# Block decay factors gathered by GpSimd and DMA in place of products on TensorE, and four more blocks transposed by DMA

## The chip, the cores and the metric

The kernel runs on one core of a Trainium2 chip. The metric is the time of one execution on the device in microseconds; lower is better. A ratio in this document is the mean time of one kernel's fast runs over the mean time of the other kernel's fast runs of the same rounds on the same chip, so it is not quite the ratio of the medians that are quoted beside it. A run is called slow here when it lies over 1.5% above the fastest of its kernel.

## The reference

A gated linear attention over 4 batches, 8 heads, 768 steps and a head size of 48, followed by an MLP on the 3072 tokens:

```python
state = alpha[:, :, t, :, None] * state + np.einsum('bhd,bhe->bhde', k[:, :, t], v[:, :, t])
y[:, :, t] = np.einsum('bhd,bhde->bhe', q[:, :, t], state)
...
h = x @ w_in                      # 3072 x 384 by 384 x 2048
r = np.maximum(h, 0.0)
g = s * (r * r) + b
return g @ w_out                  # 2048 x 384
```

`alpha` is drawn between 0.8 and 1.

## The kernel before

The sequence is cut into 24 blocks of 128 steps, six to a batch. A block takes logarithms of alpha, sums them along the block on TensorE (`cum`), and takes two exponentials, `b` and its inverse. VectorE scales q by `b` and k by the inverse. The scaled pair is transposed, on TensorE or by DMA, and gives the block's own output. A product of k and v (`KV`) updates the state. The new state is multiplied by the block's decay factor, one number for each of 384 columns, `blast`:

```python
def st_cum(n):
    la = la_sb[n % 2]
    nc.tensor.matmul(out=cum_ps, lhsT=U_bf, rhs=la[:, :, 0:D], start=True, stop=True)
    if n % NCH == NCH - 1:
        return
    laf = la.rearrange("a h d -> a (h d)")
    for p in range(NP):                      # 4 products with a column of ones
        nc.tensor.matmul(out=bl_ps[:, p : p + 1], lhsT=laf[:, 128 * p : 128 * p + 128],
                         rhs=ones_col_bf, start=True, stop=True)

def st_exp_i(n):
    nc.scalar.activation(out=binv_sb[n % 2], in_=cum_ps, func=AF.Exp, scale=-1.0)
    if n % NCH != NCH - 1:
        nc.scalar.activation(out=blast_sb[n % 2], in_=bl_ps, func=AF.Exp)

def st_vcast(n):                             # GpSimd; KV and the block's output need vp
    nc.gpsimd.tensor_copy(out=vp_sb[n % 4]..., in_=v_in[n % NIN]...)

def st_snew(n):                              # GpSimd; the next block's output needs the state
    ...
    nc.gpsimd.tensor_tensor(out=s_sb[n % 3], in0=t1_sb[n % 2], in1=bl, op=ALU.mult)
```

All these operations, and those of the MLP, are entered in a small planner in the kernel with an engine, a duration, a priority and what they read and write. The planner simulates the engines and writes the program in the order that comes out. On the chip each engine then takes its instructions in that order, whatever the real durations are.

## Time and profile before

| | before |
|---|---|
| time, median | 185.82 us (185.15 to 185.98, 3 runs) |
| span of the profiled execution | 183.4 us |
| TensorE / VectorE / ScalarE / GpSimd busy | 174.6 / 138.7 / 106.0 / 40.2 us |
| transposed on TensorE: blocks 4 to 7; by DMA | 4; 16 |

The prediction shows the main lines. Two more views matter for what came. One is VectorE's product of k by the inverse (busy us, mean ns of one, idle time before it):

```profile
L421 DVE TENSOR_TENSOR qk<-k_in,binv 128x384 bf16<-128x384 f32 x20 | 11.9, 596 | 0.1
```

The other is the list of waits: who waited, for whom, us in total, how often, and the longest.

```profile
POOL s_st L483 <- DVE s_st L472: 46.0, 9, 10.0
POOL vp L410 <- DMA v_in<-in_v_dram: 40.7, 12, 7.5
```

After the start GpSimd has two sorts of work, the state update (`s_st`) and the cast of v (`vp`), and stands idle before both. The second line says that a cast usually sits ready in the queue before its v has been loaded: the casts are early, which costs nothing, and nobody waits for them.

### The profile page before, as it was taken

Reading aid. Unit: us, or ns where it says so; the run is one execution under the profiler, and the core shown is the slowest. Engines: PE = TensorE matmul, PEld = TensorE weight load, DVE = VectorE, ACT = ScalarE, POOL = GpSimd, SP = SyncE. Lnnn points to the kernel's source line nnn. Section 1 sums busy time; section 2 is a strip of 40 time slices with the busy share of each in tenths; the row PEclk is TensorE's granted clock in tenths of the full one; section 3 lists DMA queues with packets and bytes.
Section 4 is the critical chain, followed back from the end, with each engine's and each line's share of the span. In section 5 each row is a group of like instructions: output and inputs, shape, how many; then the busy total and the mean of one; then the engine's idle time right before and its main releaser. Section 6 shows DMA issues by size and latency. Waiting matters only on the chain.

```text
span 183.4 us, 5324 instructions
## 1 busy us (share of the span) xinstructions
PE 174.6 (95%) x2133; PEld 124.2 (68%) x2135; DVE 138.7 (76%) x255; ACT 106.0 (58%) x215; POOL 40.2 (22%) x70
## 2 busy tenths in 40 slices
PE   6988896999999999999999999999999999999993
PEld 2356574767777776676776776776876776777762
DVE  2377999999899898687789688577897788544421
ACT  3437699946676565674764754853753662665400
POOL 7995032022112423110303311101230131000000
PEclk9999999999999999999999999999999999999999
DMA  5999999999999999996998979996974994101112
GB/s 154 355 295 321 361 370 323 193 178 223 201 185 199 214 183 192 205 211 156 228 169 178 211 153 215 185 228 146 210 175 103 209 194 119 46 4 43 43 43 86
DMA packets 115816, 34.42 MB, mean 188 GB/s; under 512 B 109008, under 2 KB 114256, under 8 KB 115792
## 3 DMA queue, kind: packets, MB, share of 16 engines
q1 hardware_dynamic: 98832, 29.89, 69.2%
q10 hardware_dynamic: 16896, 4.20, 15.7%
q8 instruction: 16, 0.26, 0.6%
q14 instruction: 8, 0.07, 0.1%
q0 software_dynamic: 64, 0.00, 0.0%
HBM read 25.17 MB, written 4.72 MB: 163 GB/s over the span
## 4 chain that ended last, share of the span: by engine, by line
PE 79%; DVE 8%; SPq 6%; DMA 4%; issue 1%; DVEq 0%
PE o_ps L754 32%; PE h_ps L692 31%; PE py_ps L527 5%; SPq L217 5%; PE a_ps L489 4%; DMA gt<-in_k_dram 4%; PE ct_ps L386 2%; DVE colpart L342 2%; DVE gt L707 1%; SPq L309 1%; PE ct_ps L447 1%; PE ct_ps L433 1%; DVE colsum L347 1%; DVE qk L589 1%; PE o_ps L723 1%
## 5 line engine op out<-in xcount | busy, mean ns | idle before, releaser
L692 PE MATMUL h_ps<-xd,w_in_bf 128*128 128x256 bf16 (+1 forms) x624 | 74.4, 265 | 0.1
L701 ACT ACTIVATE r<-h_ps 128x512 bf16<-128x512 f32 x96 | 56.3, 604 | 30.3 <-PE h_ps L692 22.8
L754 PE MATMUL o_ps<-w_out_bf,gt 128*128 128x384 bf16 x368 | 69.5, 326 | 1.4 <-ACT w_out_bf L318 1.3
L692 PEld LDWEIGHTS <-w_in_bf 128*128 128x128 bf16 x624 | 55.1, 97 | 11.1 <-issue 0.4
L707 DVE TENSOR_TENSOR gt<-r 128x512 bf16<-128x512 bf16 x96 | 42.7, 456 | 19.5 <-ACT r L701 18.4
L754 PEld LDWEIGHTS <-gt 128*128 128x128 bf16 x368 | 34.6, 98 | 19.4 <-issue 1.5
L498 DVE TENSOR_TENSOR am<-a_ps,mask 128x1024 bf16<-128x1024 f32 x24 | 29.3, 1221 | 2.3 <-PE a_ps L489 2.0
L483 POOL TENSOR_TENSOR s_st<-s_st,blast 128x384 bf16<-128x384 bf16 x16 | 14.6, 914 | 63.7 <-DVE s_st L472 46.0
L410 POOL CAST vp<-v_in 128x384 bf16<-128x384 f32 x20 | 12.2, 608 | 47.7 <-DMA v_in<-in_v_dram 40.7
L672 ACT ACTIVATE xd<-py_ps 128x384 bf16<-128x384 f32 x22 | 11.0, 502 | 17.8 <-PE py_ps L527 15.9
L765 DVE SCALAR_TENSOR_TENSOR o_sb<-o_ps,s_col,bias_w 128x384 f32<-128x384 f32 x23 | 14.2, 616 | 6.0 <-PE o_ps L754 5.0
L380 ACT ACTIVATE la<-a_in 128x384 bf16<-128x384 f32 x20 | 10.4, 521 | 7.3 <-DVE gt L707 4.5
L416 DVE TENSOR_TENSOR qk<-q_in,b_s 128x384 bf16<-128x384 f32 x20 | 12.5, 627 | 0.8 <-ACT b_s L402 0.7
L421 DVE TENSOR_TENSOR qk<-k_in,binv 128x384 bf16<-128x384 f32 x20 | 11.9, 596 | 0.1
L402 ACT ACTIVATE b_s<-ct_ps 128x384 f32<-128x384 f32 x20 | 9.7, 486 | 2.6 <-PE ct_ps L386 2.2
L405 ACT ACTIVATE binv<-ct_ps 128x384 f32<-128x384 f32 x20 | 9.9, 495 | 0.0
L489 PE MATMUL a_ps<-qkT 64*128 64x128 bf16 x192 | 9.5, 219 | 0.4 <-DVE am L498 0.2
L489 PEld LDWEIGHTS <-qkT 64*128 64x128 bf16 x192 | 5.5, 94 | 6.5 <-issue 5.1
L1026 PE MATMUL o_ps<-zeros 128*128 128x512 bf16 x19 | 7.7, 551 | 1.3 <-DVE zeros L235 1.3
L527 PE MATMUL py_ps<-am,vp 128*32 128x128 bf16 x352 | 8.8, 219 | 0.0
L472 DVE TENSOR_TENSOR s_st<-ct_ps,s_st 64x192 bf16<-64x192 f32 x20 | 7.0, 352 | 2.0 <-PE ct_ps L447 1.6
L527 PEld LDWEIGHTS <-vp 128*32 128x32 bf16 x384 | 6.5, 97 | 0.9 <-issue 0.6
(95 smaller groups left out, 133.4 us busy)
## 6 DMA issues: line engine op xcount, KB each, us to landing
out_dram<-o_sb SPq DMA_DIRECT2D x23, 192.0 KB, 2.5
v_in<-in_v_dram SPq DMA_DIRECT2D x20, 192.0 KB, 3.8
a_in<-in_alpha_dram SPq DMA_DIRECT2D x20, 192.0 KB, 4.1
k_in<-in_k_dram SPq DMA_DIRECT2D x20, 192.0 KB, 4.0
q_in<-in_q_dram SPq DMA_DIRECT2D x20, 192.0 KB, 3.9
wst<-in_moe_w_in_dram SPq DMA_DIRECT2D x4, 768.0 KB, 7.5
gt<-in_moe_w_out_dram SPq DMA_DIRECT2D x4, 768.0 KB, 9.2
gt<-in_alpha_dram SPq DMA_DIRECT2D x2, 384.0 KB, 4.9
```

Of the source, the lines that this page charges most:

```text
L410: nc.gpsimd.tensor_copy(out=vp_sb[n % 4].rearrange("a p (x d) -> a p x d", d=D)[:, :, 0:3:2, :], in_=v_in[n % NIN].rearrange("a (p e) d -> ...
L416: nc.vector.tensor_tensor(out=qk_sb[n % 4][:, 0, :, 0:D], in0=q_in[n % NIN], in1=b_sb[n % 2], op=ALU.mult)
L421: nc.vector.tensor_tensor(out=qk_sb[n % 4][:, 1, :, 0:D], in0=k_in[n % NIN], in1=binv_sb[n % 2], op=ALU.mult,)
L483: nc.gpsimd.tensor_tensor(out=s_sb[n % 3], in0=t1_sb[n % 2], in1=bl, op=ALU.mult)
L489: nc.tensor.matmul(out=a_ps[:, e, p, :], lhsT=qkT[64 * e : 64 * e + 64, 1, p, :], rhs=qkT[64 * e : 64 * e + 64, 0, p, :], start=True, stop ...
L498: nc.vector.tensor_tensor(out=am_sb[n % 2].rearrange("a e p t -> a (e p) t"), in0=a_ps.rearrange("a e p t -> a (e p) t"), in1=(mask2 if n ...
L527: nc.tensor.matmul(out=y_of(n)[32 * (x % 4) : 32 * (x % 4) + 32, x // 4, :], lhsT=(st[:, p, c0 : c0 + 32] if e is None else vp[:, p, c0 + ...
L692: nc.tensor.matmul(out=hp[:, i * n : (i + 1) * n], lhsT=w_in_bf[:, kk, 128 * j : 128 * (j + 1)], rhs=xd_sb[g % 3][:, kk, 0:n], start=(kk = ...
L701: nc.scalar.activation(out=r_sb[w % 2], in_=h_ps[w % 2], func=AF.Relu)
L707: nc.vector.tensor_tensor(out=gt_sb[:, s0 : s0 + m, js[0] : js[0] + len(js)].rearrange("a s j t -> a j s t"), in0=r, in1=r, op=ALU.mult,)
L754: nc.tensor.matmul(out=op[:, 0:d_model], lhsT=gt_sb[:, s0, j], rhs=w_out_bf[:, j, :], start=(j == 0), stop=(j == NJ - 1),)
L765: nc.vector.scalar_tensor_tensor(out=ots, in0=o_ps[(x // 4) % 2][:, 0:d_model], scalar=s_col, in1=bias_w, op0=ALU.mult, op1=ALU.add,)
```

## The change

The intent is to take work off TensorE. `b` of the last step in a block is already the decay factor, as one row on one partition. The change has GpSimd copy that row into another order and two small DMAs spread it over the partitions. Blocks 4 to 7 go from TensorE's transposes to DMA. The planner's constants were searched anew. The diff, cut to its core:

```diff
-GROUPS = [2, 2, 1, 1, 2, 2, 2, 2, 2, 2, 2, 2, 2]
-UNIT = 0.548
+GROUPS = [2, 2, 1, 1, 1, 1, 1, 1, 1, 1, 1, 2, 2, 2, 1, 2, 2]
+UNIT = 0.295
-NPE = 8
+NPE = 4
-NAY = 12
+NAY = 10
+NBL = 4
+TBL = 1.7
+BLP = 49.5
-CE = ["POOL", "DVE", ...]
+CE = ["ACT", "DVE", ...]
 ... (all 27 priorities in P are new, the store of block 18 goes to GpSimd's queue,
      and blast becomes four tiles of fp32 in place of two of bf16)
-        if n % NCH == NCH - 1:
+        if n % NCH == NCH - 1 or n >= NBL:
             return
 ...
+    def st_bl(n):
+        rows = slice(C - 32, C)
+        nc.gpsimd.tensor_copy(
+            out=b_row[rows, n % 2].rearrange("a e d p -> a p e d"),
+            in_=b_sb[n % 2][rows].rearrange("a (p e) d -> a p e d", e=2),
+        )
+        for e in range(2):
+            nc.gpsimd.dma_start(
+                out=blast_all[64 * e : 64 * e + D, n % 4, :], in_=b_row[C - 1 : C, n % 2, e]
+            )
 ...
+            op("ACT", 0.41, t + P["ei"], st_exp_i, n, r=["ct"], w=[("bi", i2)])
+            if not last(n):
+                op("POOL", TBL, t + BLP, st_bl, n, r=[("b", i2)], w=[("bl", s4)], lat=3.4)
```

The planner is thus told that the gather takes GpSimd 1.7 us and lands 3.4 us later.

More of the change, by code (lines that the diff above doesn't have):

```diff
@@ L16 @@
 VW = 144
-GROUPS = [2, 2, 1, 1, 2, 2, 2, 2, 2, 2, 2, 2, 2]
-UNIT = 0.548
-LEAD = {1: 116.8, 2: 316.2, 4: 55.7}
-NPE = 8
-NAY = 12
+GROUPS = [2, 2, 1, 1, 1, 1, 1, 1, 1, 1, 1, 2, 2, 2, 1, 2, 2]
+UNIT = 0.295
+LEAD = {1: 165.9, 2: 313.7, 4: 51.3}
+NPE = 4
+NAY = 10
 RING = 12
 NST = 4
-TB = 1.04
+TB = 0.88
 TW = 2.2
@@ L34 @@
 NY = 2
-NKV = 9
+NKV = 10
 NR2 = 2
+STQ = 18
+NBL = 4
+TBL = 1.7
+BLP = 49.5
 TC2 = ["DVE", "DVE"]
 VC2 = ["ACT", "ACT"]
-CE = ["POOL", "DVE", "ACT", "ACT", "ACT", "ACT", "ACT", "ACT"]
+CE = ["ACT", "DVE", "ACT", "ACT", "ACT", "ACT", "ACT", "ACT"]
 TC = dict(ACT=1.4, DVE=0.87, POOL=2.0)
@@ L42 @@
 COLD = 9.0
-P_BM, P_CS, P_BMM = -5, -166.6, 420.9
+P_BM, P_CS, P_BMM = -5, -264.9, 436.0
 P = dict(
-    ln=37.38, cum=-5.89, eb=-21.67, ei=-20.73, vc=52.19, qb=-9.21, kb=4.29, T=47.45,
-    Tc=-10.24, KV=-8.06, t1=-26.76, sn=121.36, Ay=-20.23, A=-31.59, mk=-31.84, y=-27.08,
-    ye=22.77, m1=-10.34, re=8.62, sq=-6.75, m2=-16.59, oe=-37.4, vm=-45.28, ci=-71.74,
-    co=-1313.2, ls=295.04, vn=18.84,
+    ln=60.4, cum=-21.17, eb=-43.71, ei=-25.37, vc=49.76, qb=-0.52, kb=0.09, T=60.15,
+    Tc=-13.57, KV=3.78, t1=-20.78, sn=117.05, Ay=-30.04, A=-44.0, mk=-19.93, y=-36.45,
+    ye=18.77, m1=-13.74, re=21.48, sq=1.75, m2=-13.14, oe=-42.62, vm=-2.86, ci=404.27,
+    co=-1295.27, ls=140.41, vn=85.16,
 )
@@ L288 @@
     am_sb = many("am", 2, [128, 2, NP, 128], BF16)
-    blast_all = sb.tile([128, 2, NP], BF16, name="blast")
-    blast_sb = [blast_all[:, i] for i in range(2)]
+    blast_all = sb.tile([128, 4, NP], FP32, name="blast")
+    nc.vector.memset(blast_all, 1.0)
+    b_row = sb.tile([128, 2, 2, D, NP], FP32, name="b_row")
+    blast_sb = [blast_all[:, i] for i in range(4)]
     xd_sb = many("xd", 3, [128, 3, 512], BF16)
@@ L405, in st_exp_i @@
         nc.scalar.activation(out=binv_sb[n % 2], in_=cum_ps, func=AF.Exp, scale=-1.0)
-        if n % NCH != NCH - 1:
-            nc.scalar.activation(out=blast_sb[n % 2], in_=bl_ps, func=AF.Exp)
+        if n % NCH != NCH - 1 and n < NBL:
+            nc.scalar.activation(out=blast_sb[n % 4], in_=bl_ps, func=AF.Exp)
+    def st_bl(n):
[8 more added lines that the diff above has]
+            )
     def st_vcast(n):
@@ L463, in st_t1 @@
     def st_t1(n):
-        bl = blast_sb[n % 2].unsqueeze(2).to_broadcast([128, NP, D])
+        bl = blast_sb[n % 4].unsqueeze(2).to_broadcast([128, NP, D])
         for e in range(2):
@@ L481, in st_snew @@
             return
-        bl = blast_sb[n % 2].unsqueeze(2).to_broadcast([128, NP, 96])
+        bl = blast_sb[n % 4].unsqueeze(2).to_broadcast([128, NP, 96])
         nc.gpsimd.tensor_tensor(out=s_sb[n % 3], in0=t1_sb[n % 2], in1=bl, op=ALU.mult)
@@ L584, in pair_exp_i @@
         )
-        nc.scalar.activation(out=blast_all, in_=bl2_ps, func=AF.Exp)
+        nc.scalar.activation(out=blast_all[:, 2 * m % 4 : 2 * m % 4 + 2], in_=bl2_ps, func=AF.Exp)
     def pair_mul(m, x):
@@ L776, in ostore @@
         n = first_blk[g] + tt
-        nc.sync.dma_start(out=out[n * C : (n + 1) * C, :], in_=out_sb[(x // 4) % 3])
+        eng = nc.gpsimd if n == STQ else nc.sync
+        eng.dma_start(out=out[n * C : (n + 1) * C, :], in_=out_sb[(x // 4) % 3])
     sched = Schedule()
@@ L879, in add_block @@
         op("ACT", 0.45, t + P["ln"], st_ln, n, r=[("a", ii)], w=[("la", i2)])
-        op("PE", 0.27, t + P["cum"], st_cum, n, r=[("la", i2)], w=["ct"], lat=0.16)
+        op("PE", 0.27 if n < NBL and not last(n) else 0.16, t + P["cum"], st_cum, n, r=[("la", i2)], w=["ct"], lat=0.16)
         op("ACT", 0.41, t + P["eb"], st_exp_b, n, r=["ct"], w=[("b", i2)])
-        op("ACT", 0.49, t + P["ei"], st_exp_i, n, r=["ct"], w=[("bi", i2), ("bl", i2)])
+        if n < NBL and not last(n):
+            op("ACT", 0.49, t + P["ei"], st_exp_i, n, r=["ct"], w=[("bi", i2), ("bl", s4)])
+        else:
+            op("ACT", 0.41, t + P["ei"], st_exp_i, n, r=["ct"], w=[("bi", i2)])
+            if not last(n):
+                op("POOL", TBL, t + BLP, st_bl, n, r=[("b", i2)], w=[("bl", s4)], lat=3.4)
         op("POOL", 0.5, t + P["vc"], st_vcast, n, r=[("v", ii)], w=vp, lock=True)
@@ L909, in add_pair @@
         op("ACT", 0.9, t + P["ei"], pair_exp_i, m, r=["a"],
-           w=[("bi", 0), ("bi", 1), ("bl", 0), ("bl", 1)])
+           w=[("bi", 0), ("bi", 1), ("bl", s), ("bl", s + 1)])
         op("DVE", 0.88, t + P["qb"], pair_mul, m, 0, r=[("Q", h), ("b", 0), ("b", 1)], w=qb, lock=True)
@@ L941, in finish_block @@
         if first(n):
-            op("DVE", 0.65, t + P["t1"], st_t1, n, r=[pb(n), ("bl", i2)], w=[("S", i3)])
+            op("DVE", 0.65, t + P["t1"], st_t1, n, r=[pb(n), ("bl", s4)], w=[("S", i3)])
         elif not last(n):
             op("DVE", 0.65, t + P["t1"], st_t1, n, r=[pb(n), ("S", (n - 1) % 3)], w=[("t1", i2)])
-            op("POOL", 0.85, t + P["sn"], st_snew, n, r=[("t1", i2), ("bl", i2)], w=[("S", i3)], lock=True)
+            op("POOL", 0.85, t + P["sn"], st_snew, n, r=[("t1", i2), ("bl", s4)], w=[("S", i3)], lock=True)
         rA, wA = qT, ["a"]
@@ L949, in finish_block @@
             r1, w1 = ys.pop(n - 1)
-            op("PE", 0.935, want(n - 1) + P["Ay"], st_Ay, n, r=rA + r1, w=wA + w1, lat=0.16)
+            op("PE", 0.834, want(n - 1) + P["Ay"], st_Ay, n, r=rA + r1, w=wA + w1, lat=0.16)
             yevac_op(n - 1)
@@ L974, in add_group @@
             t = w * UNIT
-            op("PE", 0.67 if m == 1 else 0.65, t + P["m1"], mm1, w,
+            op("PE", {1: 0.67, 2: 0.656, 4: 0.648}[m], t + P["m1"], mm1, w,
                r=[("xd", g % 3, x) for x in range(m)] + [("wib", js[0] // 4)],
```

## The prediction

> **What bounds the kernel now.** I read four views of the profile of before, in this order: the table of engines with the 40 slices, the chain that ended last, the groups of instructions, and the timeline of TensorE. The first tells which engine is full and when.
>
> ```profile
> PE 174.6 (95%) x2133; PEld 124.2 (68%) x2135; DVE 138.7 (76%) x255; ACT 106.0 (58%) x215; POOL 40.2 (22%) x70
> ...
> PE   6988896999999999999999999999999999999993
> ...
> DVE  2377999999899898687789688577897788544421
> ...
> POOL 7995032022112423110303311101230131000000
> PEclk9999999999999999999999999999999999999999
> DMA  5999999999999999996998979996974994101112
> ```
>
> TensorE is at 9 tenths in every slice from the eighth to the last but one (a slice is 4.6 us), at full clock; before that it has gaps and 19 filler products (7.7 us) that only keep it busy. VectorE is full as well from about 20 to 60 us. GpSimd is nearly empty after 25 us, which is what makes it a place for new work. The DMA engines are full until about 83 us. "Busy" alone does not say that TensorE sets the end, so I took the chain next:
>
> ```profile
> PE 79%; DVE 8%; SPq 6%; DMA 4%; issue 1%; DVEq 0%
> PE o_ps L754 32%; PE h_ps L692 31%; PE py_ps L527 5%; SPq L217 5%; PE a_ps L489 4%; DMA gt<-in_k_dram 4%; PE ct_ps L386 2%; DVE colpart L342 2%; DVE gt L707 1%; SPq L309 1%; PE ct_ps L447 1%; PE ct_ps L433 1%; DVE colsum L347 1%; DVE qk L589 1%; PE o_ps L723 1%
> ```
>
> 79% of 183.4 us is 145 us. In order of time the chain is loads until 18.5 us, mostly VectorE until 37.4 us, and from there TensorE to 180.3 us; the last 3 us are the eviction and the store. So after 37 us a piece of TensorE work that goes away shortens the kernel by what it took there, unless a new wait appears; work on another engine counts only where TensorE waits for it.
>
> How much TensorE time the removed pieces take cannot be read from their busy time, because matmuls overlap. It is read from start to next start in the timeline of TensorE:
>
> ```profile
> 43.89 0.67 PE L433 MATMUL ct_ps<-ident_bf,qk 128*128 128x128 bf16 x8
> 44.39 0.81 PE L754 MATMUL o_ps<-w_out_bf,gt 128*128 128x384 bf16 x4
> 45.04 0.83 PE L692 MATMUL h_ps<-xd,w_in_bf 128*128 128x128 bf16 x12
> 45.71 0.33 PE L386 MATMUL ct_ps<-la,U_bf 128*128 128x384 bf16 x1
> 45.87 0.24 PE L393 MATMUL ct_ps<-ones_col_bf,la 128*128 128x1 bf16 x4
> 46.05 0.40 PE L489 MATMUL a_ps<-qkT 64*128 64x128 bf16 x8
> ...
> 54.06 0.61 PE L433 MATMUL ct_ps<-ident_bf,qk 128*128 128x128 bf16 x8
> 54.50 0.33 PE L447 MATMUL py_ps<-vp,qk 128*128 128x96 bf16 x4
> ```
>
> Eight transposes hold TensorE for 0.50 us (43.89 to 44.39) or 0.44 us (54.06 to 54.50). Four ones-products hold it for 0.18 us here (45.87 to 46.05, with a small wait), but over all 16 such groups the median from start to next start is 0.10 us and the sum 1.8 us. A unit of the first MLP product with one block (12 matmuls of 128 columns) takes 0.67 us; with two blocks (6 of 256 columns) the median of such groups is 0.65 us.
>
> **What the Trainium skill says.** "TensorE: Matmul & The Clock Gate", section "Back-to-back issue gap", says that start to start has a floor of about 25 ns for tiny products and that a pair of weight load and matmul at 128 columns can cost about 81 ns. The trace agrees with the first (0.10 us for four one-column products) and not with the second: 12 pairs in 0.67 us are 56 ns each. "DMA: Bandwidth & Descriptors", section "Anatomy of one DMA — SWDGE (gpsimd) path", gives a DMA issued by GpSimd about 2 us whatever its size, most of it the receipt of the write. Before's two tiny GpSimd loads took 4.8 and 4.4 us, among full DMA engines, so I count 3 to 5 us for the new ones. "SBUF — State Buffer", section "SBUF: two separate sides", says that GpSimd and some VectorE operations exclude each other on a shared port, and that descriptors of GpSimd's DMAs are held up by it. The casts on GpSimd in this trace are a hint of that: 0.50 us alone and up to 0.84 us otherwise.
>
> **The change part by part.** First, blocks 4 to 7 go from TensorE transposes to DMA transposes. TensorE loses 4 x 0.45 = 1.8 us, all after 38 us and so on the path. VectorE loses four copies:
>
> ```profile
> L456 DVE COPY qkT<-ct_ps 128x1024 bf16<-128x1024 bf16 x4 | 2.7, 686 | 0.2
> ...
> L393 PE MATMUL ct_ps<-ones_col_bf,la 128*128 128x1 bf16 x64 | 3.9, 165 | 0.0
> L407 ACT ACTIVATE blast<-ct_ps 128x4 bf16<-128x4 f32 x16 | 3.1, 192 | 0.0
> ```
>
> That is 2.7 us in a stretch (38 to 56 us) where it is over nine tenths busy. The queues gain four transposes: 16 of them took 15.7% of the DMA engines' time, so 1.8 us of all 16 engines each, together 7.2 us, at a time when the engines are full with loads. ScalarE's queue issues them, 1.25 us each, 5 us more.
>
> Second, the ones-products of 16 blocks go: 16 x 0.105 = 1.7 us of TensorE on the path, with 3.1 us of ScalarE beside it. In their place GpSimd makes 16 copies of 384 values (by the casts of the same size, some 0.6 to 0.8 us) and issues 32 small DMAs (before's two occupied it 0.70 and 0.54 us). That is 16 x (0.7 + 2 x 0.5) = 27 us, so GpSimd goes from 40 to about 67 us of 182, beside TensorE. The factor is there some 4 to 6 us after its exponential instead of at once; the exponentials are given an earlier place in the new order.
>
> Third, ten groups of one block replace two such groups: 8 blocks x 4 units x 0.02 us = 0.6 us more on TensorE. The cast of the first weights moves from GpSimd to ScalarE (1.5 us, in the start, where ScalarE has room), and one store moves to GpSimd's queue so that loads do not wait behind it.
>
> Fourth, the order of everything is searched anew. In 37 to 60 us the starts of TensorE's groups leave about 2.6 us more than their columns need, later about 4 us in all. With VectorE relieved and smaller groups I expect 1.0 us of this back, and 0.3 us lost to waits for the gathered factors: 0.7 us net. This is my choice, not a reading.
>
> Sum: -1.8 - 1.7 + 0.6 - 0.7 = -3.6 us, so 185.8 - 3.6 = 182.2 us, 1.9% less.
>
> **The rivals.** One: the gathered factor comes late. The new state needs it, the next block's output product needs the state, and TensorE executes in order. For it speaks that GpSimd's queue also holds casts that wait for loads (40.7 us in all in before) and that DMA is full until 83 us. Against it: those waits were for work not yet due, and there are about 7 us of TensorE work per block to fill. If a third of 16 blocks lost 0.7 us each, the gain would shrink to nothing, 185 to 186 us.
>
> Two: DMA becomes the bound. Its queues took 85% of the span, 156 us; 7.2 us more make 163. The last loads and transposes are at 153 us in before, with pure MLP work behind them from about 157 us, so about 10 us of delay can be absorbed; only the start (block 4's loads land just before its first product at 35.3 us) has little room. It would cost 1 to 2 us: 183.5 to 184 us.
>
> Three: the old start stays the limit and the whole gain is the 2.9 us of arithmetic above: 182.9 us.
>
> Four: the new order removes most of the 6 us of small gaps. Then 179 to 180 us.
>
> **The range and the chances.** Rival three and four lie either side of my number, one and two above it. I take 180.0 to 184.4. The line of 2% lies at 182.1 us, almost at my number: 0.47 for faster by over 2%, 0.48 for the same, 0.05 for slower, which would need rival one in full and more.
>
> **What would show it.** Right: no ones-products after the pairs, 20 DMA transposes, 816 matmuls in the first MLP product, TensorE still the chain from about 37 us, and its work after that shorter by about 3 us. The output product's waits would show rival one as idle time ending in GpSimd's state update or in the small DMAs landing after over 5 us; a later last block of attention (beyond 160 us) with idle TensorE would show rival two; a TensorE that becomes dense at the same 37 us with the same small gaps shows three. I would be wrong above all if the new order changes the first 37 us, which I have left as they are.

## More of the kernel before

The experiments ran on several chips, and each has its own runs of the kernel before; a difference between two ratios is therefore often one between chips.

An operation marked `lock=True` excludes others so marked, which models a port that VectorE and GpSimd are taken to share:

```python
op("POOL", 0.5, t + P["vc"], st_vcast, n, r=[("v", ii)], w=vp, lock=True)
op("DVE", 0.48, t + P["kb"], st_kb, n, r=[("k", ii), ("bi", i2)], w=[("kb", s4)], lock=True)
...
op("POOL", 0.85, t + P["sn"], st_snew, n, r=[("t1", i2), ("bl", i2)], w=[("S", i3)], lock=True)
```

## The result, and the profile after

The changed kernel took 190.85 us in the median (190.63 to 192.15, 4 runs) against 185.9 us (185.15 to 186.85, 4 runs): a ratio of 1.0278, 95% interval 1.0212 to 1.0344. It is slower by almost 3%, where I had put 182.2 us and a chance of 0.05 on this class. A repeat on another chip gave 1.0211 (1.0165 to 1.0257).

From the page of the changed kernel: busy time, the 40 slices (4.7 us each), the chain, and three groups (busy us, mean ns, then idle time before them and its cause).

```profile
PE 172.8 (91%) x2232; PEld 124.0 (66%) x2232; DVE 139.6 (74%) x252; ACT 106.3 (56%) x200; POOL 71.1 (38%) x118
...
PE   6669987899999997999999999999969999999992
...
PEclk9999999999999999999999999999979999999999
...
PE 38%; DMA 3%; DVE 2%; POOL 2%; issue 1%; ACT 1%; ACTq 0%; DVEq 0%; POOLq 0%
...
L417 POOL COPY b_row<-b_s 32x384 f32<-32x384 f32 x16 | 17.2, 1077 | 42.4 <-ACT b_s L408 40.0
...
L500 POOL TENSOR_TENSOR s_st<-s_st,blast 128x384 bf16<-128x384 bf16 x16 | 14.2, 887 | 23.5 <-DMA blast<-b_row 10.1
...
L438 DVE TENSOR_TENSOR qk<-k_in,binv 128x384 bf16<-128x384 f32 x20 | 15.8, 792 | 0.0
```

TensorE is busy less, 172.8 us instead of 174.6, in a span that is 5.5 us longer. It has holes where it had none: in the sixteenth slice (71 to 76 us) and the thirtieth (137 to 142 us), where its granted clock falls to 7 tenths as well. The chain can be followed back only to 94 us, so its shares don't add up to 100; what is new is that within this half it runs through DMA, VectorE, GpSimd and ScalarE, where in the kernel before it ran on TensorE alone. VectorE's product of k takes 0.79 us in the mean; it took 0.596 us before.

Of the list of waits of the changed kernel, three lines:

```profile
POOL b_row L417 <- ACT b_s L408: 40.0, 12, 6.4
...
POOL vp L427 <- DMA v_in<-in_v_dram: 6.3, 3, 3.4
...
PE ct_ps L464 <- POOL vp L427: 1.9, 2, 1.8
```

GpSimd now waits for ScalarE's exponential before the copies. A cast found its v not yet loaded three times, no longer twelve: the casts come late, behind other things, and TensorE's `KV` product (`ct_ps L464`) waits twice for one, once for 1.8 us.

The hole at 137 us shows how. First GpSimd's timeline (start us, us, then the idle time before and its cause), then two lines of VectorE, then TensorE:

```profile
128.32 1.20 POOL L417 COPY b_row<-b_s 32x384 f32<-32x384 f32 x1 [1.60 <-ACT b_s L408]
129.82 1.00 POOL L422 DMA_DIRECT2D blast<-b_row  x2 [0.29 <-POOL b_row L417]
134.91 0.92 POOL L500 TENSOR_TENSOR s_st<-s_st,blast 128x384 bf16<-128x384 bf16 x1 [4.09 <-DVE qk L438]
135.89 0.99 POOL L417 COPY b_row<-b_s 32x384 f32<-32x384 f32 x1
137.17 1.06 POOL L422 DMA_DIRECT2D blast<-b_row  x2 [0.29 <-POOL b_row L417]
138.28 0.50 POOL L427 CAST vp<-v_in 128x384 bf16<-128x384 f32 x1
```

```profile
128.70 1.05 DVE L438 TENSOR_TENSOR qk<-k_in,binv 128x384 bf16<-128x384 f32 x1
...
134.26 0.55 DVE L438 TENSOR_TENSOR qk<-k_in,binv 128x384 bf16<-128x384 f32 x1
```

```profile
136.68 0.41 PE L544 MATMUL py_ps<-am,vp 128*32 128x128 bf16 x16
138.83 0.46 PE L464 MATMUL ct_ps<-vp,qk 128*128 128x96 bf16 x4 [1.75 <-POOL vp L427]
139.09 1.48 PE L771 MATMUL o_ps<-w_out_bf,gt 128*128 128x384 bf16 x4
140.37 2.42 PE L709 MATMUL h_ps<-xd,w_in_bf 128*128 128x256 bf16 x12
142.63 0.33 PE L392 MATMUL ct_ps<-la,U_bf 128*128 128x384 bf16 x1
```

The state update stands in GpSimd's queue behind the factor's DMAs and starts 4.09 us after they were issued. The next block's copy, its DMAs and only then the cast follow, 0.99 + 1.06 + 0.50 us with the gaps between, and TensorE has nothing for 1.75 us. (The profile puts the wait down to VectorE's product of k, which ended at 134.81 us. The two DMAs landed 4.4 us after their issue, at 134.2 and about 134.7 us, so without that product the update could hardly have started earlier. In the experiment g_act_pool the profile names the small DMAs at the same place, 5.98 us.) After the hole TensorE's products are slow: four that take 0.65 us elsewhere take 1.28 us from start to next start (139.09 to 140.37), and twelve that take 1.32 us take 2.26. The granted clock of that stretch is in the view by windows (window, TensorE, its weight loads, VectorE, ScalarE, GpSimd busy, then the clock):

```profile
139.00:142.60 3.60, 3.60 (x20) 2.35 (x19) 1.35 (x4) 0.60 (x1) 0.75 (x1) 0.54 0.71 131
```

It is 0.54. The Trainium skill, in "TensorE: Matmul & The Clock Gate", section "What's actually happening", says that the clock is halved after an idle window of about 3.4 us and given back after a busy one. The trace agrees with the half (0.50 in the windows 139 to 140 and 140 to 141 us), but TensorE had been idle for only 1.75 us. So this wait cost another 1.6 us here ((1.28 - 0.65) + (2.26 - 1.32)). That part doesn't come with every such hole: in g_act_pool a hole of 1.79 us at the same place left the clock at 1.00, and so did one of 1.4 us in the profile of the repeat.

VectorE's two lines, above TensorE's, show a second harm. When the copy runs beside it (128.32 to 129.52) the product of k takes 1.05 us, otherwise 0.55.

### The profile page after: what moved, and what is told of

Its sections match the earlier page's. It is cut to its first block, busy times and chain, and to the rows that moved or that the text cites. A ratio compares the mean times of both kernels' runs of the same rounds, so it can differ in the third digit from the quotient of the medians.

```text
span 188.9 us, 5578 instructions
## 1 busy us (share of the span) xinstructions
PE 172.8 (91%) x2232; PEld 124.0 (66%) x2232; DVE 139.6 (74%) x252; ACT 106.3 (56%) x200; POOL 71.1 (38%) x118
## 5 line engine op out<-in xcount | busy, mean ns | idle before, releaser
L718 ACT ACTIVATE r<-h_ps 128x512 bf16<-128x512 f32 x96 | 55.7, 599 | 38.1 <-PE h_ps L709 14.9
L709 PE MATMUL h_ps<-xd,w_in_bf 128*128 128x128 bf16 (+1 forms) x816 | 74.6, 243 | 0.7 <-ACT r L718 0.7
L771 PE MATMUL o_ps<-w_out_bf,gt 128*128 128x384 bf16 x368 | 71.0, 328 | 1.4 <-ACT w_out_bf L324 1.3
L709 PEld LDWEIGHTS <-w_in_bf 128*128 128x128 bf16 x816 | 61.3, 98 | 11.8 <-issue 2.2
L417 POOL COPY b_row<-b_s 32x384 f32<-32x384 f32 x16 | 17.2, 1077 | 42.4 <-ACT b_s L408 40.0
L422 POOL DMA_DIRECT2D blast<-b_row x32 | 16.7, 526 | 4.7 <-POOL b_row L417 4.7
L438 DVE TENSOR_TENSOR qk<-k_in,binv 128x384 bf16<-128x384 f32 x20 | 15.8, 792 | 0.0
L427 POOL CAST vp<-v_in 128x384 bf16<-128x384 f32 x20 | 10.5, 527 | 13.9 <-PE a_ps L506 7.0
L489 DVE TENSOR_TENSOR s_st<-ct_ps,s_st 64x192 bf16<-64x192 f32 x18 | 6.4, 354 | 4.0 <-PE ct_ps L464 2.0
```

What stands on the lines that cost most here:

```text
L417: nc.gpsimd.tensor_copy(out=b_row[rows, n % 2].rearrange("a e d p -> a p e d"), in_=b_sb[n % 2][rows].rearrange("a (p e) d -> a p e d", e=2),)
L422: nc.gpsimd.dma_start(out=blast_all[64 * e : 64 * e + D, n % 4, :], in_=b_row[C - 1 : C, n % 2, e])
L438: nc.vector.tensor_tensor(out=qk_sb[n % 4][:, 1, :, 0:D], in0=k_in[n % NIN], in1=binv_sb[n % 2], op=ALU.mult,)
L709: nc.tensor.matmul(out=hp[:, i * n : (i + 1) * n], lhsT=w_in_bf[:, kk, 128 * j : 128 * (j + 1)], rhs=xd_sb[g % 3][:, kk, 0:n], start=(kk = ...
L718: nc.scalar.activation(out=r_sb[w % 2], in_=h_ps[w % 2], func=AF.Relu)
L771: nc.tensor.matmul(out=op[:, 0:d_model], lhsT=gt_sb[:, s0, j], rhs=w_out_bf[:, j, :], start=(j == 0), stop=(j == NJ - 1),)
```

## The experiments

**Theory.** The loss comes from the gather on GpSimd: its place in an in-order queue, the wait for its landing, and its use of the port shared with VectorE. **Rivals:** the new order and the four additional DMA transposes cost it; or the operations are harmful only in this order. Two sorts of kernels tell these apart. Those in the changed kernel's own order leave the planner as it is and alter only what an operation emits, so that everything else stays in place. Those of the kernel before in its own order get the new operations where the old ones stood.

| run | ratio to before | 95% interval | median us (its before) |
|---|---|---|---|
| changed kernel | 1.0278 | 1.0212 to 1.0344 | 190.85 (185.9) |
| s_no_gather | 0.9874 | 0.9825 to 0.9923 | 184.32 (186.67) |
| s_dma_only | 0.9924 | 0.9881 to 0.9968 | 185.72 (186.67) |
| s_copy_only | 1.0049 | 0.9991 to 1.0108 | 187.93 (186.67) |
| o_ones | 0.9982 | 0.9937 to 1.0027 | 186.5 (186.67) |
| s_wait_only | 0.9949 | 0.9862 to 1.0036 | 185.56 (186.5) |
| s_wait_memset | 0.9923 | 0.9837 to 1.0009 | 185.56 (186.5) |
| s_wait_dma | 1.0081 | 1.0006 to 1.0156 | 187.11 (185.93) |
| g_act_pool | 1.0209 | 1.0131 to 1.0287 | 190.53 (186.5) |
| g_act_act | 1.1383 | 1.1284 to 1.1483 | 212.67 (186.5) |
| o_cast_first | 1.0078 | 0.9989 to 1.0167 | 186.4 (185.93) |
| o_after_k | 1.0149 | 1.0106 to 1.0191 | 189.17 (185.94) |
| changed kernel again | 1.0211 | 1.0165 to 1.0257 | 190.1 (185.94) |
| s_no_early_T | 1.0146 | 1.0031 to 1.0261 | 190.33 (186.47) |
| q_T | 1.0833 | 1.0739 to 1.0928 | 201.42 (186.47) |
| q_gather | 1.0303 | 1.0226 to 1.038 | 191.87 (186.47) |
| q_both | 1.1007 | 1.0886 to 1.1129 | 205.48 (186.47) |
| v_split | 1.0248 | 1.0179 to 1.0318 | 190.52 (185.93) |
| v_ones | 0.9941 | 0.987 to 1.0012 | 184.82 (185.93) |

For two runs the record's ratio is not that of the runs which it labels fast. In s_wait_only four of six runs are slow because one took only 182.67 us; its two fast runs alone make 183.78 / 186.70 = 0.984. In o_cast_first the three fast runs make 185.86 / 185.48 = 1.002.

### Is it the gather? (changed kernel's order)

Edits of `st_bl`: return at once; the copy alone; the DMAs alone from a row set once; and, in the fourth run, the ones-products and their exponentials back.

```diff
 def st_bl(n):
-    nc.gpsimd.tensor_copy(...)      # dropped in s_no_gather, s_dma_only, o_ones
-    for e in range(2):              # dropped in s_no_gather, s_copy_only, o_ones
-        nc.gpsimd.dma_start(...)
```

> The changed kernel in its own order, but the gather does nothing: no copy, no small DMAs, the factor stays what it was (wrong result on purpose). If the gather's side effects (GpSimd's time in its queue, the wait for the landing, VectorE slowed on the shared port) cost what was lost, this is 181 to 183.5 us. If the new order or the four more DMA transposes cost it, it stays at 188 us or more.

> As above but GpSimd's copy is made and only the two small DMAs are left out (wrong result on purpose). If the copy is what hurts (1.08 us in GpSimd's queue, and VectorE's product of k slowed from 0.60 to 0.79 us), most of the loss stays: 186 to 190 us. If the DMAs and their landing hurt, it is near the run without any gather, 182 to 184 us.

> As above but only the 32 small DMAs are made, from a row that is set once, without the copy (wrong result on purpose). If the landing of the DMAs is what the state update waits for, 186 to 190 us; if the copy is, 182 to 185 us.

> The changed kernel in its own order with the ones-products and the small exponentials put back in all blocks in place of the gather (right result). TensorE gets 1.7 us of work back. If the gather's side effects are the loss, 183 to 185.5 us, that is faster than the changed kernel by over 5 us although TensorE does more. If the order or the transposes are, 190 us or more.

Without any gather the kernel takes 0.9874 of before; with it, 1.0278, and 1.0211 in the repeat. The gather costs 4.0 or 3.4%, 7.5 or 6.3 us (the comparison crosses chips). The ones-products in the same order make 0.9982, about 3% faster than the change, although they give TensorE work back: they cost 1.1% (0.9982 - 0.9874, each with an interval of about 0.5% to either side), which is 2.0 us of 186.67. So the gather is the bulk of the loss, and the rival of the order falls that far. The ones-products' median, 186.5 us, is a little above the 183 to 185.5 expected of it; the order with its transposes is worth about nothing over the kernel before.

The copy alone adds 1.75%, the DMAs alone 0.5%, both together 3.4 to 4.0%. The sum of the two is 2.25%, less than both together. One reading is that the DMAs alone start at once and land early, while those behind the copy land late; the next experiments test it.

The profiles of the changed kernel and of s_no_gather show where the time goes, because TensorE has the same products in the same order in both. The `KV` product after the hole and the next `cum`, in s_no_gather:

```profile
135.00 0.34 PE L457 MATMUL ct_ps<-vp,qk 128*128 128x96 bf16 x4
...
137.14 0.33 PE L392 MATMUL ct_ps<-la,U_bf 128*128 128x384 bf16 x1
```

In the changed kernel they start at 138.83 and 142.63 us. It is behind by 0.1 us at the bias product (37.93 against 37.79), by 1.8 at 73.39, 2.1 at 101.01, 3.8 at 138.83, 5.5 at 142.63 and 5.6 in its last product (184.31 against 178.73). So the hole at 137 us and the clock after it are 3.4 of 5.6 us. The hole at 73 us is 1.1 us more: TensorE waits 1.34 us for a DMA transpose (0.21 us in s_no_gather) that was issued 0.74 us later, after a product of k of 1.06 us beside the copy instead of 0.55. Which of the gather's effects made that wait isn't shown: in o_cast_first that product takes 1.05 us as well, and the wait is 0.21 us.

(s_no_gather and s_copy_only still agreed with the reference: the stale factor is about as small as the right one, a product of 128 numbers between 0.8 and 1, some 0.9^128 = 1.4e-6.)

### What of the copy, and what of its landing? (changed kernel's order)

```diff
-        nc.gpsimd.tensor_copy(out=b_row[rows, n % 2]..., in_=b_sb[n % 2][rows]...)
+        nc.gpsimd.tensor_copy(out=...[:, 0:8], in_=...[:, 0:8])     # s_wait_only, s_wait_memset, s_wait_dma
+        nc.gpsimd.memset(dummy[:, 0:1080], 0.0)                     # s_wait_memset only
-        for e in range(2): nc.gpsimd.dma_start(...)                 # kept in s_wait_dma only
```

> The changed kernel in its own order; GpSimd copies only 8 of the 384 columns and no small DMAs are made (wrong factor on purpose). GpSimd's queue still waits at this place for ScalarE's exponential, but is not occupied. If the waiting in order is what the copy costs, this stays near the run with the copy alone (1.005 of before); if the copy's length or its use of the shared port costs, it falls to the run without any gather (0.987).

> As the run before, and after the 8 columns GpSimd sets a tile to zero, about 1.0 us long, which reads nothing (wrong factor on purpose). GpSimd is occupied as long as by the copy, but no read meets VectorE's products of q and k. If the shared port costs, VectorE's product of k is back at 0.60 us and the time at 0.987 to 0.992; if GpSimd's occupation costs, 1.00 to 1.01.

> The changed kernel in its own order; GpSimd copies only 8 columns of the row (so it waits for ScalarE's exponential as in the change) and then issues the two small DMAs (wrong result on purpose). If the landing behind the exponential is what the state update and the queue behind it wait for, 1.01 to 1.02 of before; if the copy's length or port is what makes the difference, 0.99 to 1.00, as with the DMAs alone.

Waiting in order for the exponential costs little (0.9949, with a wide interval, or 0.984), and no cost of occupying GpSimd 1.0 us longer with a write is seen on top (0.9923). The full copy instead of the 8 columns costs about 1% (1.0049 - 0.9949), of which the intervals don't make much. The profiles are clearer. VectorE's product of k, first with the copy alone, then with the tile set to zero in its place:

```profile
L434 DVE TENSOR_TENSOR qk<-k_in,binv 128x384 bf16<-128x384 f32 x20 | 16.8, 840 | 0.0
```

```profile
L436 DVE TENSOR_TENSOR qk<-k_in,binv 128x384 bf16<-128x384 f32 x20 | 11.0, 549 | 0.0
```

0.84 against 0.55 us: what slows VectorE here is a GpSimd instruction that reads, not one that only occupies GpSimd. That is what the Trainium skill says in "SBUF — State Buffer", section "Who interferes with whom": a VectorE instruction with two inputs in that memory contends with a GpSimd instruction that reads it, not with one that only writes. The trace agrees.

The DMAs behind the 8 columns make 1.0081, against 0.9924 for the DMAs that don't wait for the exponential: 1.6% for the same DMAs landing later. It is just under the 1.01 expected if the landing is what counts, and across chips.

The ratios hide one thing. Before the first gather's copy (36.5 us) the profiled executions already differ: TensorE reached the bias product at 37.3 to 37.9 us where its clock had been full, but at 39.4 us in s_copy_only, 39.1 in s_wait_dma, 40.4 in s_wait_memset and 39.8 in the repeat of the changed kernel, where it had been at 0.52 to 0.56 from 12 to 19 us. As two executions of the same changed kernel differ so, it isn't the gather. From the bias product to the end of the span, in single executions:

| run | us |
|---|---|
| changed kernel; again | 151.0; 149.6 |
| s_no_gather; o_ones | 145.1; 145.6 |
| s_wait_only; s_wait_memset | 143.7; 144.0 |
| s_copy_only | 147.0 |
| s_dma_only; s_wait_dma | 146.5; 147.1 |
| o_cast_first | 145.6 |
| g_act_pool | 151.2 |

Against the eight columns (143.7) the full copy adds 3.3 us, a write of the same length 0.3, and the DMAs add 3.4, so the copy and the landing are about equal, and both together add 5.9 to 7.3. Differences of under 1.5 us mean nothing here.

### Who makes the row? (changed kernel's order)

```diff
 def st_exp_i(n):
     nc.scalar.activation(out=binv_sb[n % 2], in_=cum_ps, func=AF.Exp, scale=-1.0)
+    nc.scalar.activation(out=b_row[rows, n % 2].rearrange("a e d p -> a p e d"),
+                         in_=cum_ps[rows].rearrange("a (p e) d -> a p e d", e=2), func=AF.Exp)
 ...
-            nc.gpsimd.dma_start(...)
+            nc.scalar.dma_start(...)          # g_act_act only
```

> The changed kernel in its own order with the row made by ScalarE as a third exponential of the last 32 rows (some 0.5 us of ScalarE) and the two DMAs still issued by GpSimd (right result). If GpSimd's copy is the main cost, this loses most of the 2.25% between the DMAs' alone and all of the gather: 0.995 to 1.005. If the landing and the order of the queue are, 1.015 to 1.03.

> As the run before, but ScalarE's queue issues the two DMAs too, so that GpSimd does nothing of the gather (right result). If GpSimd is the cause, 0.99 to 1.00. If ScalarE, which also evicts the first product of the MLP, then becomes what TensorE waits for, 1.00 to 1.02.

(The 2.25% in the first text is the sum of the two parts alone; from the DMAs alone to the whole gather it is 2.9 to 3.5%.) g_act_act missed; g_act_pool came within what was expected if the landing and the order of the queue are the cause, but it doesn't prove that. The third exponential took 0.865 us, not 0.5, though it has a quarter of the partitions of the other two (0.49 us); it writes with a stride. 16 of them are 13.8 us on ScalarE, which evicts the MLP's first product, so the run (1.0209) doesn't tell how much of the copy's cost was saved. It does show that the hole before the cast comes without any copy on GpSimd: TensorE's `KV` product waits 1.79 us at 139.93 us, and VectorE's product of k is at 0.61 us. With the DMAs on ScalarE's queue the time is 1.1383. ScalarE at one block in that run:

```profile
72.75 1.18 ACTq L425 DMA_DIRECT2D blast<-b_row  x2
73.98 0.49 ACT L692 ACTIVATE xd<-py_ps 128x384 bf16<-128x384 f32 x1 [1.25 <-issue]
```

While the queue issues two DMAs of 0.8 KB (1.18 us), the engine stands, and the eviction of the block's output behind them is late. Moving the gather there only moves the harm.

### Are the casts behind the wait the harm? (changed kernel, casts moved)

In the order that the planner gives, each cast of v is moved ahead of up to two gathers or state updates in front of it in GpSimd's queue, as far as what it overwrites allows. In o_after_k the gather is also put behind VectorE's product of k in the order, and the copy waits for that product.

```diff
+        for i in [casts of v]:
+            least = position after the last operation that the cast depends on
+            pool = [GpSimd's operations between least and the cast][-2:], gathers and updates only
+            if pool: move the cast in front of pool[0]
 ...
+        nc.gpsimd.tensor_copy(out=after_kb, in_=qk_sb[n % 4][:, 1, 0, 0:1])   # o_after_k only
```

> The changed kernel, only GpSimd's casts of v moved ahead of up to two gathers or state updates in its queue (right result). If the casts held up behind the state update's wait are the main harm, 1.00 to 1.015 of before; if the late state itself or the slowed VectorE is, 1.02 to 1.03 as the change.

> The changed kernel with the casts of v moved ahead as before, and with the gather's copy made to wait for VectorE's product of k of the same block (it reads one column of it first), so that the two don't meet (right result). VectorE's product of k should be back at 0.55 to 0.62 us from 0.73. If that meeting is most of what is left, 0.990 to 1.002 of before; if the factor's lateness is, which grows by about 1.5 us here, 1.008 to 1.025.

> The changed kernel again, on the same chip and in the same rounds as the run above: 1.022 to 1.034 of before, as at first.

Moving the casts alone, with nothing else touched, takes the ratio from 1.0278 or 1.0211 to 1.0078. The comparison crosses chips, and the intervals of the repeat and of this run just touch (1.0165 and 1.0167), so its size is uncertain: the differences are 1.3 and 2.0%, or 1.9 and 2.6% with the 1.002 of the fast runs. GpSimd at the same place:

```profile
127.65 1.00 POOL L430 DMA_DIRECT2D blast<-b_row  x2 [0.29 <-POOL b_row L425]
129.31 0.50 POOL L435 CAST vp<-v_in 128x384 bf16<-128x384 f32 x1 [0.66 <-DMA v_in<-in_v_dram]
132.44 0.90 POOL L508 TENSOR_TENSOR s_st<-s_st,blast 128x384 bf16<-128x384 bf16 x1 [2.63 <-DMA blast<-b_row]
133.41 0.97 POOL L425 COPY b_row<-b_s 32x384 f32<-32x384 f32 x1
```

The cast now lies inside the time in which the update waits for the landing, where it costs nothing. From 120 to 140 us, in the windows' view, the changed kernel and this one (TensorE busy is the second number after the window's length):

```profile
120.00:140.00 20.00, 18.25 (x217) 12.77 (x215) 15.47 (x30) 10.98 (x23) 8.95 (x13) 0.97 1.04 184
```

```profile
120.00:140.00 20.00, 20.00 (x267) 14.54 (x267) 17.09 (x32) 11.51 (x23) 7.98 (x12) 1.00 1.08 190
```

TensorE's hole and the fall of the clock are gone. From the bias product on, this execution takes as long as the one without any gather, within 0.5 us.

Letting the copy wait for the product of k brought that product back to 0.58 us, but the time was 1.0149, not better than 1.0078. (The profiled execution serves only for this duration.) By its making the factor comes later in this kernel. So the meeting on the port is real but isn't shown to be the main part of what is left; that its saving went into the later factor is likely and not shown.

### The transposes, and the old order

```diff
 def st_Tdma(n):
+    if n < 8: return                     # s_no_early_T: changed kernel's order, wrong result
 ...
-    st_T on TensorE and st_Tcopy         # q_T, q_both: kernel before, own order
+    nc.scalar.dma_start_transpose(...)
 ...
-    ones-products, exponential of them   # q_gather, q_both: kernel before, own order
+    st_bl(n) in its place
```

> The changed kernel in its own order without the DMA transposes of blocks 4 to 7, and with nothing in their place (wrong result on purpose). If they do the harm, by the landing or by delaying loads, 185 to 187 us; if the gather does it, 190 us as the changed kernel.

> The kernel before in its own order, only blocks 4 to 7 transposed by DMA (right result). TensorE loses 1.8 us and VectorE 2.7 us. If the transposes' landing (4.6 us in the median) is covered by the order, 184 us; if TensorE has to wait for it, 186 to 189 us, as the old order placed the transposes late.

> The kernel before in its own order, only the factor gathered by GpSimd and DMA (right result). If the gather's side effects do the harm whatever the order, 187 to 190 us; if they were harmful only in the new order, 183.5 to 185 us.

> The kernel before in its own order with both parts of the change (right result). If the two parts do the harm and not the new order, 187 to 191 us; if the new order does it, 182 to 184 us.

s_no_early_T gave 1.0146 with two of four runs slow; that the four early transposes cost up to a per cent is possible and not shown. In the old order the transposes are far worse than expected, 1.0833: the order left too little time for the landing. One wait of that run:

```profile
PE a_ps L493 <- DMA qkT<-qk: 10.6, 4, 4.5
```

Four waits of up to 4.5 us, at a mean clock of 0.956. The gather in the old order costs 3.0% although TensorE loses the ones-products, much as in the new order. So the harm of the gather isn't a matter of one order, and the transposes need an order made for them.

### Can another order carry it?

The planner was given what the trace shows: 1.15 us for the copy, with `lock=True`, 1.1 us for the DMAs, 4.5 us until they land. Its constants were searched again, once with the gather and once with the ones-products.

```diff
-op("POOL", TBL, t + BLP, st_bl, n, r=[("b", i2)], w=[("bl", s4)], lat=3.4)
+op("POOL", 1.15, t + BLP, st_bl_copy, n, r=[("b", i2)], w=[("brow", i2)], lock=True, lat=0.25)
+op("POOL", 1.1, t + BLP - 0.01, st_bl_dma, n, r=[("brow", i2)], w=[("bl", s4)], lat=4.5)
 ... (new constants; 2.6 us instead of 2.0 for a DMA transpose to land;
      v_ones with NBL = 24, v_split with NPE = 6)
```

> The operations of the change, with the order searched again after the planner was given what the trace shows: 1.15 us for the copy, exclusive with VectorE's products, 1.1 us for the two DMAs, 4.5 us until they land (right result; two blocks stay on TensorE). If the order planned on too short durations was the fault, 0.985 to 1.00 of before. If the gather is harmful in any order, 1.01 to 1.03.

> The DMA transposes from the fifth block on with the ones-products, order searched again in the same way (right result). TensorE has 1.7 us more than in the change. If only the gather is harmful, 0.98 to 0.995 of before, the best right version; if the planner's order doesn't hold on the chip, 1.00 or more.

v_split gave 1.0248, in the range written down for a gather that is harmful in any order, which one search can't prove. VectorE's product of k was at 0.55 us, so the port was respected, but TensorE waited elsewhere, twice about 1.5 us for ScalarE's logarithm. Better durations for the gather were not enough for this search to find a good order; whether one exists in which the gather pays stays open. v_ones, the transposes with the ones-products, is the fastest right version here, 0.9941, but its interval (0.987 to 1.0012) includes no change. No right version that I ran clearly beats the kernel before.

## Why the prediction was wrong

**The bound and TensorE's arithmetic** held. I counted 1.7 us for the ones-products; putting them back in the same order cost 2.0 us. I counted 2.9 us for all of TensorE's pieces; the changed kernel without the gather is 2.3 us faster than before (186.67 - 184.32, medians). The four transposes' share of it was not isolated in a kernel with a right result, and of the 1.0 us that I expected back from the new order nothing shows (2.9 + 1.0 would be 3.9).

**The step that failed is the fourth, "0.3 us lost to waits for the gathered factors: 0.7 us net".** In its place the runs show 6.3 to 7.5 us for the gather, and 5.6 us between the two profiled executions. It was rival one, which I priced at "185 to 186 us" in full; I gave slower by over 2% only 0.05. Three terms were missing or too small; the runs don't divide the loss among them exactly:

- *The place in the queue.* I weighed the lateness of the factor for the state alone. Behind the waiting update stand the next gather and the cast of v, and TensorE's `KV` product waits for the cast. Moving the casts alone recovered some 1.3 to 2.6%. My argument against the rival was that the casts' 40.7 us of waiting in before "were for work not yet due". The waiting was in fact the slack that kept the casts early; the change used it up (6.3 us left).
- *The port.* I named the exclusive port and took from it only a doubt about the descriptors. The copy starts when `b` is ready, which is also when VectorE's products start, and the product of k went from 0.596 to 0.792 us: 20 x 0.196 = 3.9 us of VectorE, not all of it on the path. The copy cost about 3 us more than a write in its place (147.0 against 144.0 us from the bias product on, single executions).
- *Durations.* I took 0.6 to 0.8 us for a copy of 384 values, by the casts; it takes 1.08 us. The DMAs' issue (0.53 us each) was right, and so was the landing in the median, 3.7 us after the issue where I had 3 to 5; single ones took 1.9 to 6.6. But copy, gap and DMAs hold GpSimd 1.08 + 0.29 + 1.06 = 2.4 us where the planner had 1.7, so the order was built on too little. That this made the loss isn't shown: v_split was planned with the measured durations and took 1.0248.

**Also not foreseen:** in the profiled execution the clock fell after the hole of 1.75 us and cost another 1.6 us.

**The other rivals.** DMA as the bound is not seen: the last DMA transpose was issued at 158.5 us, and TensorE is full after that. The first 37 us, of which I had warned, changed little: TensorE reached the bias product at 37.93 us instead of 37.41.

## What to carry to other kernels

In an in-order queue the cost of a new wait is paid by what stands behind it: before an operation that waits is put on an idle engine, list what else that engine serves and who waits for it. Idle time in a list of waits may be the slack that keeps that work early. And a plan or an estimate that moves work to another engine has to price the new operation from a measured duration of its own kind (strides, shared ports, landing): here the work saved was near what was computed, and the operation put in its place cost about three times as much.

## What the Trainium skill lacked or had wrong

- "TensorE: Matmul & The Clock Gate", section "Back-to-back issue gap", gives about 81 ns for a pair of weight load and matmul at 128 columns; here it is 56 ns (12 pairs in 0.67 us), which is what its formula for isolated matmuls gives.
- "DMA: Bandwidth & Descriptors", section "Anatomy of one DMA — SWDGE (gpsimd) path", gives a fixed cost of about 2 us for a DMA; among other traffic these of 0.8 KB landed 1.9 to 6.6 us after the issue, 3.7 us in the median.
- "GPSIMD Engine Reference", section "7. Performance pitfalls for Q7 kernels", prices strided reads; a strided write isn't priced there: the copy of 32 x 384 took 1.08 us where casts of 128 x 384 took 0.53 us in the same kernel. No page has a time for it on ScalarE: 0.865 us for 32 x 384 with a strided write against 0.49 us for 128 x 384 without. (That the stride is the cause was not tested by itself.)
- "DMA: Bandwidth & Descriptors", section "Issuing engines are not separate DMA queues", calls the time to initiate a DMA "usually small relative to the DMA itself"; on ScalarE's queue two DMAs of 0.8 KB took 1.18 us to issue, against 3.1 us from issue to landing in the median, and the engine stood for as long, over twice an eviction of 0.49 us.
- "TensorE: Matmul & The Clock Gate", section "What's actually happening", gives an idle window of about 3.4 us for the half clock; here a hole of 1.75 us was enough in one execution, and one of 1.79 us in another was not.
